# Slots ahead of weights, later embeddings, and squares, gates and scalings elsewhere, in a fused retention and mixture-of-experts kernel

## The chip, the cores and the metric

The kernel runs on one core of a Trainium2 chip. A core has TensorE (PE: matrix products, with its weight loads as PEld), VectorE (DVE), ScalarE (ACT), GpSimd (POOL) and SyncE (SP), which mostly issues DMAs. Each engine takes its own instructions in order and waits on semaphores for the others. The metric is the time of one execution on the device in microseconds (us); less is better.

## The reference

```
def _attn_ref(q, k, v):                       # 4 x 8 x 768 x 64
    gamma = 1.0 - 2.0 ** (-5.0 - arange(H)); scale = 1 / sqrt(D)
    for t in range(S):
        state = gamma * state + k[t] (x) v[t]
        y[t] = scale * q[t] @ state

def _moe_ref(x, expert_emb, tau, w1, w2):     # N, D, E, F = 3072, 512, 8, 1024
    xn = x / (norm(x) + 1e-6); en = expert_emb / (norm(expert_emb) + 1e-6)
    logits = xn @ en.T / tau
    expert_idx = argmax(logits, axis=1)
    probs = exp(logits - logits.max()); probs /= probs.sum() + 1e-9
    for e in range(E):
        h = maximum(x[mask e] @ w1[e], 0)
        out[mask e] = probs[expert e] * (h @ w2[e])

x = attention output, heads side by side, as (batch * sequence) x 512
```

All inputs and the output are float32.

## The kernel before

**Retention.** The recurrence is done in blocks of 256 tokens: 4 batches of 3 blocks are the 12 turns `m` of one loop (L718). k and q of a block are scaled by powers of gamma (`scale_k`, `scale_q`, on GpSimd, two blocks ahead) and transposed on TensorE (`transpose_k`, `transpose_q`, copied out by ScalarE into `kT`, `qT`). `scores` multiplies them, `masks` multiplies the scores by a causal mask on VectorE (`pm`), `inter` adds what comes from the running state and `intra` the product of `pm` and v (L410). `take` copies the result to `yT`, `rows` transposes it on VectorE and writes it to `xd` in memory in four DMAs. The buffers `pt` (two of them) take all transposes and small products.

**Routing, beside it.** One turn later `logits_products` multiplies `yT` by the normalised expert embeddings `enT`, which `expert_emb` makes in steps (norm on VectorE with a power on GpSimd, scaling, four small transposes on TensorE at L607, a copy to `enT`). The blocks are in six groups (`GROUPS`); at the end of a group `sums` and `choose` find the best expert of each token, `count` and `ranks` its slot, and `place` writes one record per token (row of x, row of the output, shifted logits) to the table `tbl` by indirect DMAs of GpSimd, one per 128 tokens (L529). Expert 0 starts early: its first 288 slots (`EARLY`) are filled from the first nine blocks alone, read to `tb` (`early_slots`), and their rows gathered from `xd` into `xge` (`early_gather`). The rest, `LATE`, are gathered into `xr0` after the last block.

**Experts.** Products are done with split operands: every float32 operand is a high part of type float32r and a low part, and three products are added (high by high, low by high, high by low). The eight weight pieces of an expert (four of w1, four of w2, 512 KB each) are loaded by SP into `raw` buffers (`load_piece`; three buffers, in order) and split by `split`: ScalarE casts the high part `whi` (L210), VectorE, sometimes GpSimd, subtracts for the low part `wlo` (L215). `LOADS` and `SPLITS` say in which blocks the first pieces are loaded and split. The rows of an expert are gathered to `xr` (`gather_rows`, one buffer), written to `xs` in memory (`write_rows`), read back in another order to `xg` (`read_quarters`), and then quarter by quarter transposed on VectorE (`x_turn`), cast on ScalarE (`xh`, L923) and subtracted (`xl`, L929, `x_low`). The norm of each row comes from `squares` on ScalarE, the factor `gt` of its output from `gates`, small steps on VectorE with a power on GpSimd and an exponential on ScalarE.

The loop over experts (L1092) has a first layer of eight tiles `ft` (12 products each, L228, then `hidden`: the activation to `hh` on ScalarE, the low part `hl` on VectorE) and a second layer: experts up to 4 in four column groups (L939), turned by `y_turn` and written to `og` by sixteen small DMAs (`out_rows`, L951) in the next expert's first layer; experts 5 to 7 in three row groups (L981). `finish` multiplies by `gt` and GpSimd scatters the rows to the output (L963). Splits, loads, squares and gates of the next expert are placed by hand at numbered tiles: the order in which the code is written is the order on every engine. For expert 0, the late rows pass the first layer as rows (L1014, output `hr`) and are then transposed.

## Time and profile before

| what | us |
|---|---|
| three timed runs | 452.30, 455.42, 456.49 (median 455.42) |
| the profiled execution | 450.94 |
| its span, first to last instruction | 449.1 |
| TensorE busy | 411.2 |
| VectorE, ScalarE, GpSimd busy | 255.5, 173.8, 168.7 |

The mean granted TensorE clock was 0.975 of the full one. Busy time of TensorE is modelled and overlaps between products, so a full stage doesn't mean that the array is at its peak. A stage is best read by who ended TensorE's waits in it, and the clock of a stage by its own row. Times in the rows are counted from the first instruction.

### The profile page before, as it was taken

The numbers are of one execution on the slowest core, as the hardware profiler recorded it, in microseconds if no ns is written. First come the engines' busy times: TensorE is split into PE (matmuls) and PEld (weight loads), VectorE is DVE, ScalarE is ACT, GpSimd is POOL, SyncE is SP. The second block draws the span as 40 slices with busy tenths as digits, with TensorE's granted clock in tenths as the row PEclk, the third lists the DMA queues.
The fourth block names the chain that finished last, engine by engine and source line by source line (L and its number), as shares of the span: only waits on it lengthen the run. The fifth ranks groups of instructions, "written<-read, shape, count | busy, mean of one in ns | idle before, by whom it ended". The sixth has DMA issues, their size and how long they took to land.

```text
span 449.1 us, 11335 instructions
## 1 busy us (share of the span) xinstructions
PE 411.2 (92%) x4540; PEld 367.0 (82%) x4540; DVE 255.5 (57%) x543; ACT 173.8 (39%) x315; POOL 168.7 (38%) x171
## 2 busy tenths in 40 slices
PE   7889889998859979997999999999998997999993
PEld 4778767877636978896899999999998987989982
DVE  3454745655862925565856585378467558666410
ACT  3314333334342515345346346156237326525300
POOL 1743356665645242072440172143135065012011
PEclk9989999999996999999899999999999999999998
DMA  9998878888583468649886968778788697864001
GB/s 238 274 227 217 224 196 228 222 217 200 131 228 112 99 165 234 151 122 279 233 267 176 229 220 243 165 254 268 177 242 273 178 290 256 257 203 138 0 26 47
DMA packets 97966, 88.75 MB, mean 198 GB/s; under 512 B 11148, under 2 KB 79644, under 8 KB 97904
## 3 DMA queue, kind: packets, MB, share of 16 engines
q1 hardware_dynamic: 92832, 74.85, 62.6%
q0 software_dynamic: 4928, 13.04, 8.4%
q8 instruction: 37, 0.61, 0.6%
q14 instruction: 25, 0.20, 0.2%
q10 hardware_dynamic: 144, 0.05, 0.1%
HBM read 65.27 MB, written 18.87 MB: 187 GB/s over the span
## 4 chain that ended last, share of the span: by engine, by line
PE 38%; DMA 16%; SPq 15%; DVE 10%; issue 10%; POOL 6%; ACT 4%; POOLq 0%; DVEq 0%; ACTq 0%
SPq L951 8%; PE py L410 5%; DMA xg<-xs 5%; PE py L981 5%; PE psc L228 4%; PE pt L330 4%; PE pst L228 4%; DMA xr<-xd,gi 4%; PE psc L357 4%; DVE wlo L215 3%; PE py L228 3%; DMA xs<-xr 2%; PE psc L939 2%; ACT whi L210 2%; SPq L912 2%
## 5 line engine op out<-in xcount | busy, mean ns | idle before, releaser
L215 DVE TENSOR_TENSOR wlo<-raw,whi 128x1024 fp32r<-128x1024 f32 x61 | 73.8, 1213 | 24.4 <-ACT whi L210 23.6
L963 POOL DMA_INDIRECT out_dram<-og,si x29 | 35.8, 1234 | 118.5 <-DVE og L956 101.7
L210 ACT CAST whi<-raw 128x1024 fp32r<-128x1024 f32 x64 | 65.6, 1043 | 6.2 <-POOL si L556 5.3
L366 DVE TENSOR_TENSOR pm<-psc,cst 128x512 f32<-128x512 f32 x48 | 30.9, 686 | 34.8 <-PE psc L357 34.8
L923 ACT CAST xh<-xt 128x384 fp32r<-128x384 f32 (+4 forms) x28 | 14.5, 522 | 73.2 <-DVE xt L922 73.2
L318 POOL TENSOR_TENSOR hl<-wlo,cst 128x512 f32<-128x512 f32 x22 | 22.9, 1062 | 51.1 <-PE pt L451 29.5
L559 POOL DMA_INDIRECT xr<-xd,gi x26 | 34.7, 1336 | 8.5 <-issue 5.5
L228 PE MATMUL pst<-xl,whi 128*128 128x384 f32 (+5 forms) x96 | 32.9, 343 | 4.0 <-DVE xl L929 4.0
L357 PE MATMUL psc<-qT,kT 64*64 64x128 f32 x768 | 35.1, 282 | 1.2 <-DVE qT L346 0.9
L247 POOL TENSOR_TENSOR r<-r,half 128x4 f32<-128x4 f32 (+1 forms) x9 | 8.9, 993 | 67.1 <-DVE r L246 67.1
L228 PE MATMUL pst<-xh,whi 128*128 128x384 f32 (+5 forms) x96 | 32.7, 341 | 1.3 <-ACT whi L210 1.2
L228 PE MATMUL pst<-xh,wlo 128*128 128x384 f32 (+5 forms) x96 | 32.4, 338 | 0.0
L529 POOL DMA_INDIRECT tbl<-zt,sloti x24 | 24.7, 1028 | 14.1 <-issue 5.8
L357 PEld LDWEIGHTS psc<-qT,kT 64*64 64x64 f32 x768 | 25.2, 136 | 5.3 <-DVE parts L459 1.5
L228 PE MATMUL py<-xh,whi 128*128 128x384 f32 (+5 forms) x84 | 28.5, 339 | 0.0
L228 PE MATMUL py<-xl,whi 128*128 128x384 f32 (+5 forms) x84 | 28.4, 338 | 0.0
L228 PE MATMUL py<-xh,wlo 128*128 128x384 f32 (+5 forms) x84 | 28.3, 337 | 0.0
L939 PE MATMUL psc<-hh,whi 128*128 128x288 f32 (+4 forms) x80 | 27.5, 344 | 0.0
L922 DVE STREAM_TRANSPOSE xt<-xg 128x416 f32<-128x416 f32 (+1 forms) x28 | 15.5, 573 | 21.0 <-DMA xg<-xs 20.1
L939 PE MATMUL psc<-hl,whi 128*128 128x288 f32 (+4 forms) x80 | 27.2, 340 | 0.0
L939 PE MATMUL psc<-hh,wlo 128*128 128x288 f32 (+4 forms) x80 | 27.2, 339 | 0.0
L228 PE MATMUL psc<-xh,whi 128*128 128x384 f32 (+5 forms) x76 | 25.4, 334 | 0.0
(207 smaller groups left out, 1019.4 us busy)
## 6 DMA issues: line engine op xcount, KB each, us to landing
raw<-in_moe_w_dram SPq DMA_DIRECT2D x46, 512.0 KB
raw<-in_moe_w_dram SPq DMA_DIRECT2D x28, 256.0 KB
xd<-x SPq DMA_DIRECT2D x48, 128.0 KB
...
```

Of the source, the lines that this page charges most:

```text
L210: nc.scalar.copy(out=hv, in_=rv)
L215: eng.tensor_tensor(out=lv, in0=rv, in1=hv.bitcast(F32), op=ALU.subtract)
L228: nc.tensor.matmul(acc[:, :w], a[:, f], x[:, kt, cols], start=(n == 0), stop=(n == 3 * KT - 1))
L318: return eng.tensor_tensor(out=dst[:, h], in0=src[m % 3][:, h, s], in1=w[:, h], op=ALU.mult)
L357: nc.tensor.matmul(psc[a][u * 64:(u + 1) * 64, j], kTs[m][a * D:(a + 1) * D, sk, j, u * 64:(u + 1) * 64], q_cols(m, a, j, u), start=True, ...
L366: i = nc.vector.tensor_tensor(out=pm, in0=psc[a], in1=C("mask")[:, sk * P:(sk + 1) * P].unsqueeze(1).broadcast_to([P, KT, P]), op=ALU.mult)
L410: nc.tensor.matmul(pys[m][u][o * D:(o + 1) * D, j], lhsT, rhs, start=first, stop=True, skip_group_check=True)
L529: i = nc.gpsimd.indirect_dma_start(out=tbl[:, :], out_offset=bass.IndirectOffsetOnAxis(ap=sloti[:, n:n + 1], axis=0), in_=zt[:, n], in_off ...
L559: nc.gpsimd.indirect_dma_start(out=xr[:n, j, :], out_offset=None, in_=xd[:rows_, :], in_offset=bass.IndirectOffsetOnAxis(ap=gi[:n, e, at:a ...
L939: nc.tensor.matmul(acc[:, :c], a[:, f], x[:, kt, :c], start=(n == 0), stop=(n == 3 * FT - 1))
L951: nc.sync.dma_start(out=og[h * Q:(h + 1) * Q, :n, i * P:(i + 1) * P], in_=yt[i * Q:(i + 1) * Q, h:nb:NQ].rearrange("p n t a -> p n (t a)"))
L963: i = nc.gpsimd.indirect_dma_start(out=out[:, :], out_offset=bass.IndirectOffsetOnAxis(ap=si[:n, e, j:j + 1], axis=0), in_=og[:n, j, :], i ...
```

## The change

It moves instructions and changes a few engines. Nothing is computed differently.

- **Embeddings:** the first steps of `expert_emb` run at the ends of blocks 0 and 1, the transposes in block 2, where the logits of blocks 0 and 1 are both made.
- **Slot writes:** `place` takes 2, then 3, then 4 columns a block instead of 2 and then 4.
- **Low parts of weights** in blocks 9 to 11 come after `choose`, `intra` and `take`; one goes to GpSimd in block 10. A fourth `raw` buffer; `LOADS` and `SPLITS` move one load and drop one split.
- **First rows of expert 0:** their transposes stand behind both `intra` of block 11.
- **After the last block:** slots are written before the last rows; the slots of the late rows and of experts 1 and 2 are read before any further weight is loaded; the first weight of expert 1 waits for the gather of the late rows.
- **Expert 0's second layer** does three column groups before the late rows instead of two.
- **Experts:** squares in the second layer of the expert before (at its first two groups), gates in the expert's own first layer, five splits in the first layer and three in the second (was four and four), the last two quarters of the next rows ahead of a split, output scaling on ScalarE, the gather of the expert after next at the second group for all experts.

TensorE between the retention and expert 0 (`pt` with `parts` are block 11's sums, `xge` the transposes of the gathered rows, `py` the products with `pm`). Before:

```order
L469 MATMUL pt<-parts,cst_61 32x32 x4
L577 MATMUL pst_2512<-ident,xge 128x128 x2
L577 MATMUL pst_2512<-ident,xge 128x32
L577 MATMUL pst_2518<-ident,xge 128x128 x2
L577 MATMUL pst_2518<-ident,xge 128x32
L577 MATMUL pt<-ident,xge 128x128 x2
L577 MATMUL pt<-ident,xge 128x32
L577 MATMUL pt<-ident,xge 128x128 x2
L577 MATMUL pt<-ident,xge 128x32
L410 MATMUL py_2428<-pm_2485,wlo 64x128
L410 MATMUL py_2428<-pm_2487,wlo 64x128
```

After:

```order
L412 MATMUL py_2427<-pm_2440,wlo 64x128
L412 MATMUL py_2427<-pm_2442,wlo 64x128
L579 MATMUL pst_2562<-ident,xge 128x128 x2
L579 MATMUL pst_2562<-ident,xge 128x32
L579 MATMUL pst_2568<-ident,xge 128x128 x2
L579 MATMUL pst_2568<-ident,xge 128x32
L579 MATMUL pt<-ident,xge 128x128 x2
L579 MATMUL pt<-ident,xge 128x32
L579 MATMUL pt<-ident,xge 128x128 x2
L579 MATMUL pt<-ident,xge 128x32
L233 MATMUL psc_2595<-xh,whi 128x288
```

The eight transposes stood between the sums and the products with `pm`; now the last products stand ahead of them, and the first layer's product with `whi` comes right behind.

SP's queue after the last block (`xd` is the write of block 11's rows, `tb` a read of slots, `raw` a weight piece, `TENSOR_LOAD` the reading of an expert's number). Before:

```order
L440 DMA xd<-x 256x1x128 x4
L169 TENSOR_LOAD cnti
L169 ISA x2
L188 ISA
L188 DMA raw<-in_moe_w_dram 128x1024
L1173 TENSOR_LOAD cnti
L1173 ISA x2
L186 ISA
L186 DMA raw<-in_moe_w_dram 64x1024
L186 ISA
L186 DMA raw<-in_moe_w_dram 64x1024
L857 DMA tb<-tbl 128x10
```

After:

```order
L172 TENSOR_LOAD cnti
L172 ISA x2
L838 ISA
L838 DMA tb<-tbl 128x4x10
L172 TENSOR_LOAD cnti
L172 ISA x2
L838 ISA
L838 DMA tb<-tbl 128x4x10
L1166 TENSOR_LOAD cnti
L1166 ISA x2
L191 ISA
L191 DMA raw<-in_moe_w_dram 128x1024
```

Three parts of two weights stood ahead of the first read of slots; now that read stands ahead of these rows, the two others in them, and the first weight comes last.

ScalarE in the first layer of expert 1 (`hh` are its activations, `sq` squares of expert 2's rows before, `whi` casts of weights, `zx` the exponential of the gates). Before:

```order
L234 ACTIVATE hh<-pst_3186 128x416
L234 ACTIVATE hh<-py_3218 128x416
L210 CAST whi<-raw 128x8x4x32
L262 ACTIVATE sq,ssq<-xr 128x512 x2
L234 ACTIVATE hh<-py_3235 128x416
L262 ACTIVATE sq,ssq<-xr 128x512
L262 ACTIVATE sq,ssq<-xr 32x512
L234 ACTIVATE hh<-psc_3261 128x416
L210 CAST whi<-raw 128x8x4x32
L234 ACTIVATE hh<-psc_3285 128x416
L234 ACTIVATE hh<-pst_3310 128x416
L210 CAST whi<-raw 128x1024
```

After:

```order
L215 CAST whi<-raw 128x8x4x32
L239 ACTIVATE hh<-pst_3168 128x416
L215 CAST whi<-raw 128x8x4x32
L239 ACTIVATE hh<-py_3200 128x416
L239 ACTIVATE hh<-py_3228 128x416
L215 CAST whi<-raw 128x8x4x32
L239 ACTIVATE hh<-psc_3243 128x416
L239 ACTIVATE hh<-psc_3272 128x416
L215 CAST whi<-raw 128x8x4x32
L282 ACTIVATE zx<-ze 128x32
L239 ACTIVATE hh<-pst_3290 128x416
L215 CAST whi<-raw 128x1024
```

The squares are gone from between the activations; the exponential, now of expert 1's own gates, stands a tile earlier.

The diff (`after` adds a dependency of one instruction on another):

```diff
@@ -51,4 +51,4 @@
 FILL = 512
-LOADS = (8, 8, 9, 9, 10, 10, 11, 11)
-SPLITS = (9, 9, 10, 10, 11, 11)
+LOADS = (8, 8, 9, 9, 9, 11, 11, 11)
+SPLITS = (9, 9, 10, 10, 11)
 STRIDE = 3200
@@ -143,3 +143,3 @@
     wp = ctxw.enter_context(tc.tile_pool(name="wp", bufs=9))
-    rp = ctxw.enter_context(tc.tile_pool(name="rp", bufs=3))
+    rp = ctxw.enter_context(tc.tile_pool(name="rp", bufs=4))
     hp = ctxw.enter_context(tc.tile_pool(name="hp", bufs=1))
@@ -167,2 +167,5 @@
 
+    def after(i, o):
+        tc.add_manual_dep(i.ins, o.ins.name, SYNC, reason="pace")
+
     def load_expert(s):
@@ -170,3 +173,3 @@
 
-    def load_piece():
+    def load_piece(behind=None):
         g = nload[0]
@@ -187,3 +190,5 @@
         elif j < 4:
-            nc.sync.dma_start(out=r, in_=w1r[ds(e * DM + j * P, P), :])
+            i = nc.sync.dma_start(out=r, in_=w1r[ds(e * DM + j * P, P), :])
+            if behind is not None:
+                after(i, behind)
         else:
@@ -332,5 +337,2 @@
 
-    def after(i, o):
-        tc.add_manual_dep(i.ins, o.ins.name, SYNC, reason="pace")
-
     def transpose_k(m, s, ps=None, copy=nc.scalar.copy):
@@ -558,3 +560,3 @@
     def gather(xr, n, j, e, at, rows_=NT):
-        nc.gpsimd.indirect_dma_start(
+        return nc.gpsimd.indirect_dma_start(
             out=xr[:n, j, :], out_offset=None, in_=xd[:rows_, :],
@@ -749,3 +751,3 @@
             nc.gpsimd.tensor_copy(out=zt[:, :, :2], in_=C("ids").rearrange("p (n o) -> p n o", o=2))
-        n = 4 if m >= NM - 3 else 2
+        n = 2 if m < 7 else 3 if m < 9 else 4
         place(ready[:n])
@@ -759,7 +761,7 @@
             transpose_k(m + 1, 1)
-        if m == 1:
+        if m == 2:
             next(emb_steps)
-        if m:
-            pl = logits_products(m - 1)
-            logits_rows(m - 1, pl)
+        for i in () if m < 2 else (0, 1) if m == 2 else (m - 1,):
+            pl = logits_products(i)
+            logits_rows(i, pl)
         if nxt:
@@ -787,4 +789,3 @@
             state_sums(m + 1)
-        if m == 0:
-            next(emb_steps)
+        if m < 2:
             next(emb_steps)
@@ -792,4 +793,4 @@
             nc.vector.memset(xge, 0.0)
-        for low in lows:
-            low(nc.vector if nxt else nc.gpsimd)
+        if m == NM - 2:
+            lows.pop()(nc.gpsimd)
         if m == NM - 1:
@@ -797,4 +798,2 @@
             run_all(add_counts(done))
-            for kt in range(KT):
-                rows_T(xge, EROWS, kt, slice(0, EARLY), bank(f"pst{kt}") if kt < 2 else None)
         intra(m, 1)
@@ -810,2 +809,7 @@
         take(m)
+        if m == NM - 1:
+            for kt in range(KT):
+                rows_T(xge, EROWS, kt, slice(0, EARLY), bank(f"pst{kt}") if kt < 2 else None)
+        for low in lows:
+            low()
         for _ in range(LOADS.count(m)):
@@ -843,4 +847,3 @@
     run_all(add_counts(g))
-    rows(m)
-    run(12)
+    run(9)
     pr = count(g)
@@ -850,2 +853,3 @@
     place(range(span(g).start, span(g).stop))
+    rows(m)
     for _ in range(9):
@@ -853,7 +857,5 @@
         run(1)
-    load_expert(1)
-    load_piece()
-    load_piece()
     nc.sync.dma_start(out=tb[:, 0, 3], in_=tbl[EARLY:CAPS[0], :])
     slots(1)
+    slots(2)
     for _ in sort_steps:
@@ -863,6 +865,6 @@
     split()
-    load_piece()
-    slots(2)
     for j, n in EROWS:
         square(xge, n, j, j)
+    run(12)
+    split()
     run(DF)
@@ -955,3 +957,3 @@
         o = og[:n, j]
-        nc.vector.tensor_scalar(out=o, in0=o if src is None else src, scalar1=gt[:n, e, j:j + 1], scalar2=None, op0=ALU.mult)
+        nc.scalar.activation(out=o, in_=o if src is None else src, func=AF.Copy, scale=gt[:n, e, j:j + 1])
         put_rows(e, j, n, og)
@@ -989,3 +991,3 @@
     indices(P, 0, slice(3, 4))
-    gather(xr0, P, 0, 0, 3)
+    late_rows = gather(xr0, P, 0, 0, 3)
     indices(P, 1, slice(0, NG))
@@ -994,3 +996,6 @@
     tokens(P, 1, slice(0, NG))
-    for dt in range(2):
+    load_piece(late_rows)
+    for _ in range(3):
+        load_piece()
+    for dt in range(3):
         acc = layer2(0, dt, hh0, hl0, EARLY)
@@ -1001,3 +1006,2 @@
     split()
-    load_piece()
     square(xr0, P, 0, 3)
@@ -1018,10 +1022,8 @@
             split()
-            load_piece()
             run_all(gsteps)
     read_quarters(1)
-    acc = layer2(0, 2, hh0, hl0, EARLY)
-    split()
     load_piece()
-    y_turn(2, acc, yt0, EARLY)
-    for f in range(2):
+    load_piece()
+
+    def turn_hidden(f):
         ps = pt_()
@@ -1033,3 +1035,8 @@
         nc.vector.tensor_tensor(out=hl0[:, kk, late], in0=o, in1=hh0[:, kk, late].bitcast(F32), op=ALU.subtract)
+
+    turn_hidden(0)
+    split()
+    load_piece()
     acc = layer2(0, 3, hh0, hl0, EARLY)
+    turn_hidden(1)
     split()
@@ -1049,7 +1056,2 @@
     squares(1)
-    gsteps = gates_of(1)
-    next(gsteps)
-    split(nc.gpsimd)
-    load_piece()
-    run_all(gsteps)
     indices(P, 2, slice(0, NG))
@@ -1071,15 +1073,13 @@
             lo()
-            load_piece()
         elif i == 1:
             x_low(e, 1)
-            lo = split_cast()
             x_turn(e, 2)
-            lo()
+            lo = split_cast()
             x_low(e, 2)
-            load_piece()
-        else:
             x_turn(e, 3)
-            split()
+            lo()
+        else:
             x_low(e, 3)
-            load_piece()
+            split()
+        load_piece()
 
@@ -1109,3 +1109,3 @@
                 nc.gpsimd.drain()
-            if ft % 2 == 0:
+            if ft in (0, 1, 3, 5, 6):
                 split()
@@ -1114,13 +1114,10 @@
                 out_rows(pend[1], pend[2], ft, pend[3])
-            if nxt:
-                if ft in (2, 3):
-                    squares(e + 1, ft - 2)
-                if ft == 3:
-                    read_quarters(e + 1)
-                if ft == 4:
-                    gsteps = gates_of(e + 1)
-                    next(gsteps)
-                if ft >= 6:
-                    for _ in range(4):
-                        next(gsteps, None)
+            if nxt and ft == 3:
+                read_quarters(e + 1)
+            if ft == 1:
+                gsteps = gates_of(e)
+                next(gsteps)
+            if ft > 2:
+                for _ in range(3):
+                    next(gsteps, None)
             if ft == FT - 2 and c % P:
@@ -1146,8 +1143,6 @@
                     finish_two()
+                if dt < 2:
+                    squares(e + 1, dt)
                 if dt < 3:
                     next_x(e + 1, dt)
-                else:
-                    split()
-                    load_piece()
-                    run_all(gsteps)
                 if dt == 1:
@@ -1161,9 +1156,7 @@
                 if nxt:
+                    if j < 2:
+                        squares(e + 1, j)
                     next_x(e + 1, j)
-                    if j == 0:
+                    if j == 1:
                         next_rows(e + 2)
-                    if j == 2:
-                        split()
-                        load_piece()
-                        run_all(gsteps)
                 finish(e, j, n, og, acc[:n])
```

## Rows read from the trace of the kernel before

**Rows 1.** Waits of TensorE over the whole span: line and tile, who ended the wait, us in total, how often, the longest.

```profile
PE pst L577 <- DMA xge<-xd,gi: 5.0, 2, 4.7
PE pst L228 <- DVE xl L929: 4.0, 4, 1.3
...
PE py L939 <- DVE hl L235: 2.7, 4, 1.4
PE pt L577 <- DMA xr<-xd,gi: 1.8, 1, 1.8
```

**Rows 2.** Busy time by stage: from and to (us), the length, then busy us and instructions of TensorE, its weight loads, VectorE, ScalarE and GpSimd, the mean granted TensorE clock (1.00 is 2.4 GHz), the share of the DMA engines and what they moved. The stages are: the end of block 1; from block 11's sums to the first layer of expert 0; the second layer of expert 0; experts 1, 2, 4, 5, 6 and 7.

```profile
23.00:31.00 8.00, 6.16 (x133) 5.21 (x133) 5.40 (x14) 1.17 (x2) 4.05 (x4) 0.79 1.07 257
130.00:143.14 13.14, 8.11 (x93) 5.47 (x89) 4.94 (x17) 3.69 (x6) 6.79 (x6) 0.61 0.66 220
157.40:187.00 29.60, 27.23 (x158) 24.23 (x157) 13.30 (x33) 9.24 (x19) 7.82 (x10) 0.94 0.76 203
187.00:230.36 43.36, 40.00 (x193) 36.86 (x192) 28.65 (x56) 21.95 (x42) 21.02 (x19) 0.96 0.73 205
230.36:265.78 35.42, 35.42 (x194) 35.42 (x193) 21.13 (x42) 15.41 (x29) 8.76 (x8) 1.00 0.76 211
300.76:336.35 35.59, 34.39 (x193) 34.07 (x193) 22.50 (x46) 15.47 (x27) 11.99 (x9) 1.00 0.83 233
336.35:371.81 35.46, 34.09 (x169) 30.34 (x169) 21.65 (x41) 15.49 (x27) 15.54 (x16) 1.00 0.83 250
371.81:408.42 36.61, 34.09 (x170) 30.34 (x169) 25.02 (x43) 18.76 (x31) 7.91 (x7) 1.00 0.69 214
408.42:442.10 33.68, 33.68 (x169) 30.20 (x167) 10.57 (x17) 5.81 (x10) 3.67 (x3) 1.00 0.16 53
```

**Rows 3.** Timeline of TensorE, then of VectorE, at blocks 1 and 2: start and length in us, line, operation, tiles and shape, how many merged, and in brackets the idle time before and what ended it.

```profile
24.50 0.44 PE L607 MATMUL pt<-ident,xge 8*128 8x8 f32 x4 [1.03 <-ACT kT L340]
...
26.32 0.66 PE L330 MATMUL pt<-ident,hh 128*128 128x128 f32 x4
26.90 0.71 PE L357 MATMUL psc<-qT,kT 64*64 64x128 f32 x8
...
30.95 0.65 PE L330 MATMUL pt<-ident,hh 128*128 128x128 f32 x4
...
37.47 0.45 PE L357 MATMUL psc<-qT,kT 64*64 64x128 f32 x8
...
39.88 0.66 PE L330 MATMUL pt<-ident,hh 128*128 128x128 f32 x4
...
22.95 0.15 DVE L249 RECIPROCAL r<-r 8x1 f32<-8x1 f32 x1 [3.48 <-POOL r L247]
```

**Rows 4.** Timeline of TensorE, then of VectorE, at the end of block 9 and the start of block 10.

```profile
115.17 0.18 PE L496 MATMUL pt<-cum,ones 128*128 128x16 f16 x1 [0.70 <-DVE zt L481]
115.78 0.17 PE L498 MATMUL pt<-oh,tri 128*128 128x16 f16 x1 [0.43 <-DVE oh L489]
...
112.45 2.36 DVE L215 TENSOR_TENSOR wlo<-raw,whi 128x1024 fp32r<-128x1024 f32 x2 [1.13 <-ACT whi L210]
```

**Rows 5.** Timeline of TensorE between block 11 and expert 0, then of VectorE, then of SP's DMA queue, a step of the chain that ended last (start, length, what), and a line of the page's groups (count, busy us, mean ns of one, idle before).

```profile
130.10 0.27 PE L469 MATMUL pt<-parts,cst 128*32 128x32 f32 x8
135.06 0.47 PE L577 MATMUL pst<-ident,xge 128*128 128x128 f32 x1 [4.69 <-DMA xge<-xd,gi]
...
139.16 1.98 PE L410 MATMUL py<-pm,wlo 64*64 64x128 f32 x32
...
143.14 0.40 PE L228 MATMUL psc<-xh,whi 128*128 128x288 f32 x1
...
130.05 1.29 DVE L366 TENSOR_TENSOR pm<-psc,cst 128x512 f32<-128x512 f32 x2
...
127.30 1.09 SPq L191 DMA_DIRECT2D raw<-in_moe_w_dram  x2
...
130.47 5.82 DMA xge<-xd,gi
...
L529 POOL DMA_INDIRECT tbl<-zt,sloti x24 | 24.7, 1028 | 14.1 <-issue 5.8
```

**Rows 6.** Timeline of TensorE, the products of expert 0's late rows: the first, the ninth and the last of 24.

```profile
167.07 0.77 PE L1014 MATMUL py<-whi,xh 128*128 128x512 f32 x1
...
170.49 0.39 PE L1014 MATMUL py<-wlo,xh 128*128 128x512 f32 x1
...
173.96 0.39 PE L1014 MATMUL py<-wlo,xh 128*128 128x512 f32 x1
```

**Rows 7.** Timeline of ScalarE in the first layer of expert 1.

```profile
206.40 0.63 ACT L262 ACTIVATE sq<-xr 32x512 bf16<-32x512 f32 x1 [1.08 <-DMA xr<-xd,gi]
```

**Rows 8.** Timeline of SP's DMA queue, then of VectorE, in the second layer of expert 3.

```profile
285.58 2.96 SPq L912 DMA_DIRECT2D xg<-xs  x4
...
292.35 1.11 DVE L922 STREAM_TRANSPOSE xt<-xg 128x416 f32<-128x416 f32 x2 [3.10 <-DMA xg<-xs]
...
302.14 1.22 DVE L215 TENSOR_TENSOR wlo<-raw,whi 128x1024 fp32r<-128x1024 f32 x1 [1.54 <-ACT whi L210]
303.29 0.56 DVE L929 TENSOR_TENSOR xl<-xt,xh 128x392 fp32r<-128x392 f32 x1
```

**Rows 9.** Timeline of VectorE at the end of the program.

```profile
442.19 0.75 DVE L956 TENSOR_SCALAR og<-py,gt 128x512 f32<-128x512 f32 x1 [4.82 <-PE py L981]
```

8 lines of the change are left out of this document (4 added, 4 removed).

## The prediction

> **What bounds the kernel now.** I read the waits of TensorE first [rows 1], then its busy time and granted clock by stage [rows 2], and last the timeline around each wait [rows 3 to 8]. The reader is to see that TensorE sets the end: in the stages of experts 2 and 7 it is busy for the whole stretch [rows 2], and elsewhere each wait names another engine or a transfer. The idle time is in few places: the first gathered rows of expert 0 (5.0 us), the low parts of the next expert's rows `xl` (4.0), the low parts of the hidden layer `hl` (2.7), the late rows of expert 0 (1.8) [rows 1]. Four of the stages have a mean granted clock under 1: it stood at its lower level, 1.2 GHz, for part of the stretch, after TensorE had been waiting [rows 2]. So a wait that goes may give back more than its own length. The profiled execution took 450.94 us with a span of 449.1; the median of the runs is 455.42, 4.5 above it. I make the sum in differences and take it off the median.
>
> **A. Embeddings one block later.** In block 0 VectorE starts the norm of the embeddings and then stands 3.48 us until GpSimd's power returns; the first masks of block 1 are queued behind it. TensorE then idles 1.03 us before the embedding transposes at 24.50 and goes on with the transposes of q at 26.32 [rows 3]. The changed kernel drops all of that from block 1: 26.32 - 24.50 + 1.03 = 2.8 us. Then the clock: scores to state products took 30.95 - 26.90 = 4.05 us, and the same instructions 39.88 - 37.47 = 2.41 us in the next block [rows 3], while the mean clock of this stretch was 0.79 [rows 2]. If TensorE isn't idle before, 1.6 us more. What is added: block 2 now has the embedding transposes, the wait for `enT` behind two masks, and the products of two blocks instead of one, which share two buffers. In block 1 the stretch from the embedding transposes to the end of the products took 26.32 - 24.50 = 1.8 us with its wait, which bounds the addition from above; nothing to 1.8, and I take 1.1, since four of the products stood in block 2 already. Net -3.3 (ends: -4.4 and -1.0; the lower one if the loads, which fill the DMA engines to a share of 1.07 in this stretch [rows 2], hold block 2 instead).
>
> **B. Low halves behind the choice.** At block 9 two low halves hold VectorE for 2.36 us and `choose` follows them; TensorE's counts wait 0.70 and 0.43 us for it [rows 4]. In the new order the choice is ahead. The halves now push the masks of block 10 instead, but by less than they pushed the counts. -1.1 (0 to -1.3).
>
> **C. First rows of expert 0.** TensorE ends block 11's sums at 130.10, gets the gathered rows at 135.06 after 4.69 us of idling, transposes them until 139.16, at the lower clock (0.61 in this stretch [rows 2]), does the 64 products with `pm` until 143.14 and starts the first layer [rows 5]. After the change the products come first. They need the second masks, which end at 130.05 + 1.29 = 131.3, a wait that block 11 hid so far: +1.0. Then 4.0 us of products and, at the full clock, 12 transposes: four of the size 128x128 take 0.66 us [rows 3], four of the 12 are narrow, so 1.8 us. 131.3 + 4.0 + 1.8 = 137.1 against 143.14: -6.0. The casts of `yT` and `xh` on ScalarE and the low parts on VectorE run a step behind the transposes, as the first layer takes them quarter by quarter. The gather must have landed by 135.3. The last of the three landed 5.82 us after its issue, at 136.3, with two raw loads issued from 127.30 on, just ahead of it [rows 5]. These loads are gone from there, and the queue of GpSimd has two slot writes less ahead of the gathers, 1.03 us each [rows 5]; both together need to win only 1.0 us. -6.0 (ends: -6.0 and -2.0, the latter if it lands no sooner than before and the clock falls again).
>
> **D. Late rows of expert 0.** The wait for `xr0` is 1.8 us [rows 1] and after it the clock is low: the first eight of 24 products of the late rows took 170.49 - 167.07 = 3.42 us, the other fifteen steps 173.96 - 170.49 = 3.47, or 0.231 each [rows 6]. Eight at that pace are 1.85: 1.6 us lost. The change puts a third output column group (24 matmuls) ahead of these rows, reads the slots ahead of the weights on SP's queue, and starts the whole chain earlier because of C. -3.4 (ends: -3.4, 0). The four weights of expert 1 now wait for the gather of `xr0` and stand ahead of the rows `xs`, `xg` of expert 1 on SP. No row shows that these rows still land in time; 1.0 us below and a rival are for that.
>
> **E. Expert 1.** Its stage takes 43.36 us, that of expert 2 35.42 for 408 columns instead of 416 [rows 2], so 36.1 would do: 7.2 us too many. ScalarE stands in the first layer for squares of rows that the gather has not brought: the last, at 206.40, waited 1.08 us for its rows [rows 7], and the activations behind it in ScalarE's order waited too; `hl` follows from them, and TensorE waits for `hl` [rows 1]. The squares move to the second layer of the expert before, where their rows landed long ago, the gates to the expert's own first layer. -7.2 (to -3.5 if part of the clock's loss stays).
>
> **F. Experts 4, 5 and 6.** Stage times 35.59, 35.46 and 36.61 against 33.68 for the undisturbed last one with 384 columns (34.4 for 392) [rows 2]: 1.2 + 1.8 + 2.9 = 5.9 us. The reason: `xg` reached VectorE only at 292.35, and the last `xl` came at 303.29 behind a low half that itself waited 1.54 us for ScalarE [rows 8], while TensorE was in the next expert since 300.76. The change helps twice: `xl` of the last quarter goes ahead of its split, and VectorE loses the output scalings and one split there. -5.9 (to -2).
>
> **ScalarE's new work.** Four scalings per expert. A square of 512 elements took 0.63 us there [rows 7], VectorE 0.75 for the last scaling out of PSUM [rows 9]; I bound the new one by half and by twice the square and take 0.63, the row on its own engine. Four of them and four squares, 5.0 us, lie beside a second layer that is about half of a stage of 35: nothing on the path, and -0.1 at the end. The Trainium skill speaks against this edit: ScalarE: Activation LUTs, "Rules for kernel authors", wants multiplications on VectorE, and its timing formula with one pointer operand gives, as an estimate from that page, 0.71 us for 512 elements. The 0.63 of the row is near that. By that rule the edit costs what the last rival below says; by the row it is free as long as ScalarE has room, and it is busy for about half of a stage or less [rows 2].
>
> **Sum.** 3.3 + 1.1 + 6.0 + 3.4 + 7.2 + 5.9 = 26.9. I put 2 against it, 1.0 for expert 1's rows and 1.0 for waits that surface when the rest moves: -25. 455.4 - 25 = **430** us, about 426 for an execution like the profiled one.
>
> **Rivals.** *Next rows late as before.* SP is in order: in the first layer it issues 16 small copies, raw loads that wait for a free buffer, `xs`, `xg`; `xg` was issued at 285.58 only [rows 8]. The diff adds one more raw load ahead of it and moves the gather of the expert after next behind the squares. If F is lost and half of E: 455.4 - 25 + 5.9 + 3.6 = 440. For it: that queue. Against: fewer waits for the squares, a fourth raw buffer, and `xl` no longer last on VectorE. *Expert 1's rows land late*, behind four weight loads on SP: as in the first rows of expert 0, 4.7 us of waiting and 1.6 of clock at its start, 436. *Weights late.* One piece less is split ahead of each expert. If each of seven second layers waits 3 us for a split, 21 us come back: 451, no change to speak of. Against: ScalarE and VectorE have room, and the last split stands two tiles ahead of the end of the first layer. *Slower: a loop over ScalarE.* Squares stand ahead of the casts `xh`, the next gather waits for the squares to free its tile, its rows go through `xs` and `xg`, and the next casts wait for those. If the loop takes longer than an expert, every boundary waits. From `xg` to the end of the last `xl` the old order took 303.29 + 0.56 - 292.35 = 11.5 us, with its waits, and TensorE lost about 1.2 us with `xg` 300.76 - 292.35 = 8.4 us ahead of the next expert [rows 2, 8]. The change is slower than before when the six boundaries from expert 1 on lose over 27 / 6 = 4.5 us each; at 11.5 us that is with `xg` landing under 5.1 us ahead. At 6 us each: 455.4 - 25 + 36 = 466. Against: the squares no longer wait for a gather, so the loop starts earlier.
>
> **How the numbers follow.** Forecast 0.62, next rows late 0.16, expert 1 late 0.10, weights late 0.07, loop over ScalarE 0.05. Lower end: all terms whole, no new wait, and a median that lies like the lowest run: 424. Upper end: the first two rivals and the short ends of A, C and D, 445; the last two stay out. About 1% is what a measurement of this kernel can tell from no change. Faster by over 1% (the first three): 0.88; within 1%: 0.07; slower: 0.05.
>
> **What the profile after would show.** No half-clock stretch in block 1 (A); counts of block 10 without a wait (B); first layer of expert 0 some 10 us earlier with no wait for `xge` but one for `pm` (C); no wait for `xr0` (D); stage of expert 1 near 36 us (E); no wait for `xl` at the later boundaries (F). The forecast is wrong if TensorE waits for `xl` at expert 1 or at every boundary, or for `whi` or `wlo` in the second layers.

## The result and the profile after

The changed kernel took 436.4 us (median of 4 runs) against 454.3 for the kernel before in the same session (455.42 in the runs shown above): a ratio of 0.956, interval 0.948 to 0.965. Ratios here and below are of the fast runs alone; two of the four timed runs, 439.51 and 439.62, lie over 1.5% above the fastest, and the profiled one is the first of them. A second session, on a chip where both were slower, gave 445.5 against 466.0, 0.952 (0.945 to 0.960). So the change gives 4 to 5%, 18 to 22 us, where 25 were forecast; 430 was too low, the range held.

The profiled execution after took 439.51 us, its span 437.7. TensorE's waits in it, to be held against [rows 1] (line and tile, who ended the wait, us in total, how often, the longest):

```profile
PE pt L500 <- DVE oh L491: 2.4, 1, 2.4
...
PE pst L233 <- ACT xh L925: 1.4, 1, 1.4
PE pst L233 <- DVE wlo L220: 1.4, 2, 0.7
...
PE pst L233 <- DVE xl L931: 1.0, 3, 0.5
```

The waits for gathered rows, 5.0 and 1.8 us in [rows 1], and that for `hl`, 2.7, are gone, and that for `xl` fell from 4.0 to 1.0. New are 2.4 us for `oh`, a step of the choice at the end of block 11, 1.4 for `xh` and 1.4 for low halves `wlo`. The stages, as in [rows 2]: from the sums of block 11 to the first layer of expert 0; second layer and late rows of expert 0; experts 1, 2, 4, 5 and 6.

```profile
130.00:140.50 10.50, 7.53 (x94) 4.92 (x90) 6.84 (x16) 2.17 (x5) 7.51 (x8) 0.66 0.88 257
156.25:183.88 27.63, 25.67 (x158) 22.90 (x156) 13.41 (x32) 8.96 (x20) 7.04 (x10) 1.00 0.83 211
183.88:222.22 38.34, 37.36 (x193) 35.82 (x193) 20.62 (x40) 20.76 (x41) 11.54 (x12) 1.00 0.79 217
222.22:259.35 37.13, 36.32 (x194) 35.35 (x193) 22.99 (x45) 20.42 (x36) 13.25 (x13) 1.00 0.85 232
294.33:330.03 35.70, 34.88 (x193) 34.09 (x193) 23.72 (x47) 20.56 (x34) 11.35 (x12) 1.00 0.85 244
330.03:363.59 33.56, 33.56 (x169) 30.38 (x169) 20.02 (x37) 18.16 (x32) 9.47 (x10) 1.00 0.86 251
363.59:397.16 33.57, 33.57 (x169) 30.39 (x168) 19.76 (x35) 17.44 (x30) 9.88 (x9) 1.00 0.88 251
```

Expert 1 fell from 43.36 to 38.34, experts 4 to 6 from 107.66 to 102.83. Expert 2 rose from 35.42 to 37.13. The first stretch still runs at a mean clock of 0.66, where it was 0.61 before.

Each run below leaves its own trace; one stage of it tells more than its time. For the retention (block 0 to the start of block 11) took 115.5 us before, 115.7 after, and 116.0 to 128.1 in twelve other traces that hardly differ there, and that spread hides anything under some 5 us. Much of it goes with the chip: 124.7 to 128.1 in the four traces of the one on which `again` ran, 116.0 to 120.7 in the eight of two others. So stages are compared, each counted from its own start.

| trace | blocks 0 to 3 | sums to first layer | first layer of 0 | to expert 1 | expert 1 | experts 2 to 6 | sums to the end |
|---|---|---|---|---|---|---|---|
| before | 44.6 | 13.0 | 14.2 | 29.7 | 43.3 | 178.1 | 319.0 |
| after | 45.6 | 10.4 | 15.8 | 27.6 | 38.3 | 174.9 | 307.6 |
| again | 43.5 | 5.7 | 15.2 | 27.4 | 38.3 | 172.9 | 300.6 |
| held_low | 45.1 | 5.7 | 14.5 | 27.1 | 39.6 | 171.7 | 299.1 |
| rows_first | 42.9 | 11.9 | 14.5 | 27.0 | 39.4 | 171.7 | 305.1 |
| no_wait | 44.0 | 6.6 | 15.3 | 26.1 | 37.4 | 174.0 | 299.9 |
| emb_early | 45.1 | 5.7 | 15.2 | 29.0 | 39.8 | 171.7 | 302.1 |
| squares_early | 42.8 | 10.6 | 16.2 | 26.8 | 38.3 | 171.7 | 304.4 |
| gates_back | 43.6 | 6.9 | 14.5 | 26.8 | 38.3 | 178.2 | 305.3 |
| sq_gates_before | 44.0 | 9.2 | 16.4 | 26.9 | 44.1 | 171.7 | 309.0 |
| finish_vector | 47.7 | 9.4 | 16.1 | 27.5 | 38.3 | 187.1 | 319.4 |
| x_order | 43.3 | 10.1 | 16.8 | 27.4 | 39.2 | 178.7 | 312.7 |
| chain | 43.0 | 9.7 | 15.8 | 27.6 | 38.3 | 171.7 | 303.7 |
| best | 43.5 | 5.7 | 14.5 | 26.1 | 37.0 | 171.7 | 295.7 |

The columns are us, from the starts of TensorE's instructions: first scores of block 0 to those of block 4; block 11's sums to the first layer of expert 0; that layer; its second layer and late rows; expert 1; experts 2 to 6 together; and all from block 11's sums to the last instruction. By the last column the change is worth 11.4 us behind the retention in its first trace and 18.3 in `again` (on another chip; the kernel before has one trace only), and nothing is seen of it in the retention.

### The profile page after: what moved, and what is told of

Its sections match the earlier page's. It is cut to its first block, busy times and chain, and to the rows that moved or that the text cites. A ratio compares the mean times of both kernels' runs of the same rounds, so it can differ in the third digit from the quotient of the medians.

```text
span 437.7 us, 11314 instructions
## 1 busy us (share of the span) xinstructions
PE 408.4 (93%) x4540; PEld 365.6 (84%) x4540; DVE 243.2 (56%) x517; ACT 191.5 (44%) x343; POOL 157.6 (36%) x169
## 4 chain that ended last, share of the span: by engine, by line
PE 47%; DMA 13%; issue 12%; SPq 11%; DVE 8%; ACT 4%; POOL 2%; POOLq 0%; DVEq 0%; ACTq 0%
PE py L412 8%; SPq L953 5%; PE pt L335 5%; PE py L233 5%; PE psc L359 5%; PE pst L233 5%; PE psc L233 5%; PE py L983 4%; PE psc L983 4%; DMA xr<-xd,gi 4%; DMA xg<-xs 3%; DMA xs<-xr 3%; PE pst L384 2%; DVE wlo L220 2%; DMA raw<-in_moe_w_dram 2%
## 5 line engine op out<-in xcount | busy, mean ns | idle before, releaser
L220 DVE TENSOR_TENSOR wlo<-raw,whi 128x1024 fp32r<-128x1024 f32 x63 | 76.6, 1218 | 22.5 <-ACT whi L215 21.4
L965 POOL DMA_INDIRECT out_dram<-og,si x29 | 29.4, 1015 | 154.7 <-ACT og L958 100.3
L368 DVE TENSOR_TENSOR pm<-psc,cst 128x512 f32<-128x512 f32 x48 | 30.9, 686 | 39.7 <-PE psc L359 39.6
L924 DVE STREAM_TRANSPOSE xt<-xg 128x416 f32<-128x416 f32 (+1 forms) x28 | 15.8, 582 | 47.7 <-DMA xg<-xs 47.7
L531 POOL DMA_INDIRECT tbl<-zt,sloti x24 | 24.9, 1039 | 14.7 <-DVE sloti L522 8.8
L925 ACT CAST xh<-xt 128x384 fp32r<-128x384 f32 (+4 forms) x28 | 14.5, 520 | 29.8 <-DVE xt L924 29.8
L233 PE MATMUL psc<-xh,wlo 128*128 128x384 f32 (+5 forms) x76 | 25.8, 339 | 0.0
L233 PE MATMUL psc<-xl,whi 128*128 128x384 f32 (+5 forms) x76 | 25.8, 339 | 0.0
L434 ACT COPY yT<-py 128x512 f32<-128x512 f32 x24 | 12.9, 589 | 27.1 <-PE py L412 25.5
L941 PE MATMUL psc<-hh,whi 128*128 128x416 f32 (+4 forms) x72 | 24.6, 341 | 0.0
```

The costliest lines, as they stand in the source:

```text
L220: eng.tensor_tensor(out=lv, in0=rv, in1=hv.bitcast(F32), op=ALU.subtract)
L233: nc.tensor.matmul(acc[:, :w], a[:, f], x[:, kt, cols], start=(n == 0), stop=(n == 3 * KT - 1))
L368: i = nc.vector.tensor_tensor(out=pm, in0=psc[a], in1=C("mask")[:, sk * P:(sk + 1) * P].unsqueeze(1).broadcast_to([P, KT, P]), op=ALU.mult)
L531: i = nc.gpsimd.indirect_dma_start(out=tbl[:, :], out_offset=bass.IndirectOffsetOnAxis(ap=sloti[:, n:n + 1], axis=0), in_=zt[:, n], in_off ...
L941: nc.tensor.matmul(acc[:, :c], a[:, f], x[:, kt, :c], start=(n == 0), stop=(n == 3 * FT - 1))
L965: i = nc.gpsimd.indirect_dma_start(out=out[:, :], out_offset=bass.IndirectOffsetOnAxis(ap=si[:n, e, j:j + 1], axis=0), in_=og[:n, j, :], i ...
```

## The experiments

All start from the changed kernel, unless said. Ratios are to the kernel before.

**The same kernel again** (`again`, no edit).

> The changed kernel itself once more. If the waits found in its first trace belong to the kernel, they come again at the same places: 2.4 us of TensorE before block 11's counts, about 1.6 us ahead of the first product of expert 1 and 1.6 us more for xl in its first tile, 0.95 us for a low half of a weight (wlo) in the first tile of experts 2 and 4. If they are chance, they move. Time 431 to 440 us, as its four runs so far.

Measured: 445.5 us, ratio 0.952. The wait for `xh` ahead of expert 1 came again (1.2 us), that for `xl` too (1.0); 2.4 us for `oh` and the low half at expert 2 did not, so these two differ between executions of the same code; at expert 4 a stop of 0.7 us stands at the same product again. What decides about `oh`, the next run shows.

**Low half on VectorE** (`held_low`).

```
         if m == NM - 2:
-            lows.pop()(nc.gpsimd)
+            held = lows.pop()
...
             run_all(ranks(done, pr))
+            held()
             place(range(span(done).start, span(done).stop))
```

> The low half that the change gives to GpSimd in block 10 runs on VectorE instead, in block 11 behind the ranks. Theory: this GpSimd subtraction (2.35 us) holds VectorE's instruction w of the choice, which took 2.78 us instead of 0.19, and so TensorE's counts; without it the counts come at once, the first layer of expert 0 starts near 137 instead of 140.5, its first products no longer run at half the clock (1.8 us), and the time falls by 4 to 5.5 us. Rival: the gathered rows xge, which landed at 134.51, only take the place of that wait, and the clock falls all the same: 0.5 to 2 us less.

VectorE, then GpSimd, then TensorE of the changed kernel at the end of block 11 (`w` and `oh` are steps of the choice, `wlo` the low half):

```profile
131.46 0.19 DVE L483 TENSOR_TENSOR zt<-pt,m 128x32 f32<-128x32 f32 x1
131.68 2.78 DVE L486 SCALAR_TENSOR_TENSOR w<-zt,cst 128x32 f32<-128x32 f32 x1
...
134.72 0.19 DVE L491 TENSOR_TENSOR oh<-w,wmn 128x32 f16<-128x32 f32 x1
```

```profile
132.06 2.35 POOL L220 TENSOR_TENSOR wlo<-raw,whi 128x1024 fp32r<-128x1024 f32 x1
```

```profile
132.41 0.19 PE L498 MATMUL pt<-cum,ones 128*128 128x32 f16 x1
134.97 0.19 PE L500 MATMUL pt<-oh,tri 128*128 128x32 f16 x1 [2.37 <-DVE oh L491]
...
135.14 1.99 PE L412 MATMUL py<-pm,wlo 64*64 64x128 f32 x32
137.06 1.79 PE L579 MATMUL pst<-ident,xge 128*128 128x128 f32 x6
...
140.50 0.61 PE L233 MATMUL psc<-xh,whi 128*128 128x288 f32 x1
```

`w` took 2.78 us and ended at 134.46, less than 0.1 us after GpSimd's subtraction. TensorE stood 2.37 us, the next 32 products took 2 us at half the clock (1.1 at the full one, 131.38) and so did the transposes. In the traces of `chain`, `squares_early` and `x_order`, where GpSimd began a little later, it was `oh` that took 2.7 to 3.0 us; in `again`, `no_wait` and `emb_early`, where it had ended before the choice, nothing was held. `w`, `oh` and the subtraction each read two operands from SBUF, the engines' on-chip memory. An instruction with only one operand there was not held, as `gates_back` shows, VectorE first and then GpSimd:

```profile
136.15 0.19 DVE L483 TENSOR_TENSOR zt<-pt,m 128x32 f32<-128x32 f32 x1
136.37 1.38 DVE L486 SCALAR_TENSOR_TENSOR w<-zt,cst 128x32 f32<-128x32 f32 x1
```

```profile
135.34 2.36 POOL L220 TENSOR_TENSOR wlo<-raw,whi 128x1024 fp32r<-128x1024 f32 x1
```

`zt`, whose `pt` lies in PSUM, the memory that TensorE writes to, ran in 0.19 us within the subtraction; `w` was held until its end. In the kernel before the same was to be seen, and missed: `r<-r,ssq` took 2.13 us beside such a subtraction, at 193.30. `held_low`, VectorE and then TensorE:

```profile
142.89 0.19 DVE L486 SCALAR_TENSOR_TENSOR w<-zt,cst 128x32 f32<-128x32 f32 x1
```

```profile
143.66 0.18 PE L500 MATMUL pt<-oh,tri 128*128 128x32 f16 x1
...
144.86 1.15 PE L579 MATMUL pst<-ident,xge 128*128 128x128 f32 x6
...
147.03 0.40 PE L233 MATMUL psc<-xh,whi 128*128 128x288 f32 x1
```

From the sums to the first layer it is 5.7 us instead of 10.4, and the first layer, at the full clock, 14.5 instead of 15.8: 6.0 less. But in `again`, on the same chip, GpSimd was early, and there it is 5.7 too. So the time, 446.2 us (0.957), is that of `again`: the edit takes away a loss that the changed kernel has in some executions (whole in four of the nine other traces that keep this code, in part in two), of 5 to 6 us when whole. The Trainium skill, SBUF — State Buffer, section "Who interferes with whom", says that VectorE with two SBUF inputs and a GpSimd instruction that reads SBUF exclude each other for a whole instruction; these traces agree.

**Rows first** (`rows_first`, from `held_low`): `rows_T` of `xge` again right behind `add_counts`, ahead of both `intra`.

> From the run with the low half on VectorE: the transposes of expert 0's gathered rows stand again ahead of the last products of the retention. Theory (term C without GpSimd's hold): TensorE waits for the gathered rows behind the sums, 3 to 4.5 us, and the clock falls behind that wait: the stretch from the last scores to the second layer of expert 0, 25.3 to 25.6 us in the two runs with the low half on VectorE, takes 4 to 6 us more. Rival: the gather lands as the masks end, and the order gives under 1.5 us.

```profile
131.54 0.27 PE L471 MATMUL pt<-parts,cst 128*32 128x32 f32 x8
134.18 0.33 PE L579 MATMUL pst<-ident,xge 128*128 128x128 f32 x1 [2.37 <-DMA xge<-xd,gi]
135.63 0.33 PE L579 MATMUL pst<-ident,xge 128*128 128x128 f32 x1 [1.12 <-DMA xge<-xd,gi]
137.04 1.17 PE L579 MATMUL pst<-ident,xge 32*128 32x32 f32 x4 [1.08 <-DMA xge<-xd,gi]
...
139.86 1.99 PE L412 MATMUL py<-pm,wlo 64*64 64x128 f32 x32
```

TensorE waits 2.37, 1.12 and 1.08 us for the three gathers, and the products with `pm` come behind at half the clock. From the sums to the first layer it is 11.9 us against 5.7: 6.2 more, where term C had 6.0. The time, 439.7 us on another chip, has a ratio of 0.961 against 0.957 for `held_low`; the intervals overlap, so the 6 us are shown by the stage alone.

**No wait of the weights** (`no_wait`): `load_piece(late_rows)` becomes `load_piece()`.

> The first weight of expert 1 no longer waits for the gather of the late rows; nothing else. Theory: with the wait, the DMA engines stand nearly idle until 158 (share 0.26 from 145 to 158) and then carry the weights and the rows of expert 1 at once, so that its rows xg land at 182.5, too late by some 3 us. Without it they land 2 to 4 us earlier and the time falls by 2 to 3 us; the late rows, which landed 6 us ahead of their use, still come in time. Rival: SP's queue and the rows' own way through memory set xg, not the weights: no change, or the late rows come late: up to 2 us more.

SP, VectorE and TensorE ahead of expert 1, first of `again`, the same chip, then of `no_wait`:

```profile
166.97 0.36 SPq L191 DMA_DIRECT2D raw<-in_moe_w_dram  x1
...
182.19 2.50 SPq L914 DMA_DIRECT2D xg<-xs  x4
```

```profile
189.53 1.10 DVE L924 STREAM_TRANSPOSE xt<-xg 128x416 f32<-128x416 f32 x2 [2.61 <-DMA xg<-xs]
```

```profile
190.82 0.46 PE L233 MATMUL pst<-xh,whi 128*128 128x416 f32 x1 [1.19 <-ACT xh L925]
```

```profile
162.91 0.35 SPq L191 DMA_DIRECT2D raw<-in_moe_w_dram  x1
...
180.06 2.38 SPq L914 DMA_DIRECT2D xg<-xs  x4
```

```profile
186.87 1.10 DVE L924 STREAM_TRANSPOSE xt<-xg 128x416 f32<-128x416 f32 x2 [0.29 <-DMA xg<-xs]
```

```profile
189.13 0.35 PE L233 MATMUL pst<-xh,whi 128*128 128x416 f32 x1
```

Counted from the start of expert 0's second layer (163.38 and 163.04), the first weight is issued 3.7 us earlier, `xg` 1.8, and VectorE waits 0.29 us for it instead of 2.61; TensorE goes on at 189.13 without a wait. Way to expert 1 and its stage: 63.5 us instead of 65.8. In time 444.5 against 445.5, inside the intervals. `best` against `chain`, below, shows the stages once more: 63.1 against 65.9.

**Embeddings early** (`emb_early`): first steps at the end of block 0 and transposes in block 1, logits of one block a turn, as before.

> Only the embeddings go back: first steps at the end of block 0, transposes and products in block 1. The prediction had 3.3 us for this part, so 3.3 us more. What the trace of the changed kernel shows: block 1 gave back 2.2 us, but block 2 took 3.05 more, of which 1.5 for the transposes and products and 1.55 at half the clock behind a stall of TensorE's own queue. So this part is worth 0 to 1.5 us: with it undone, 0 to 1.5 us more in the stretch of blocks 1 and 2.

Blocks 0 to 3 took 45.1 us; with the embeddings late 42.8 to 47.7 in twelve traces, seven of them under 43.7. The expectation held: 1 us or so, no more than one stall of TensorE's own queue, which is what this text calls a stop in which the profile shows nothing waited for ("issue"). One trace cannot tell 1 us from none here. The time, 449.3, has a ratio of 0.961 (0.955 to 0.966). In it 2.8 us are a wait for `xh` ahead of expert 1, whose first products then run at half the clock.

**Squares early** (`squares_early`). In this kernel the gates of an expert read sums of squares of the next one, which changes the output; the amount of work is the same.

```
+            if nxt and ft in (2, 3):
+                squares(e + 1, ft - 2)
...
-                if dt < 2:
-                    squares(e + 1, dt)
...
-                    if j < 2:
-                        squares(e + 1, j)
                     next_x(e + 1, j)
-                    if j == 1:
+                    if j == 0:
                         next_rows(e + 2)
```

> Of the changed kernel only the squares go back into the first layer of the expert before (its third and fourth tile), with the gather after next at the first row group for experts 5 to 7; the gates stay. Theory (term E of the prediction): in expert 1's first layer ScalarE then stands for rows that the gather has not brought (issued about 7 us into the stage, landed 15 us into it), the activations and hl behind it come late, and the stage takes 4 to 6 us more than the 38.3 of the changed kernel. Where later gathers land after those tiles too, 0 to 2 us more at each of experts 2 to 4. Together 4 to 10 us more. Rival: expert 1's stage was cured by its rows coming earlier, not by the place of the squares: under 2 us more.

Expert 1's stage: 38.34 us, to the hundredth as in the changed kernel. The theory of term E fell: with the gates late, the place of the squares gives nothing there.

**Gates back** (`gates_back`), and **squares and gates as before** (`sq_gates_before`, that and the squares, and all gates in the first layer of the expert before).

```
     squares(1)
+    gsteps = gates_of(1)
+    next(gsteps)
+    split(nc.gpsimd)
+    load_piece()
+    run_all(gsteps)
     indices(P, 2, slice(0, NG))
...
-            if ft in (0, 1, 3, 5, 6):
+            if ft in (0, 1, 3, 5, 6)[e == 1:]:
...
-            if ft == 1:
+            if ft == 1 and e > 1:
```

The last two lines are of `gates_back` alone.

> From the changed kernel, only ahead of expert 1: the gates of expert 1 and one low half of a weight on GpSimd stand again between its squares and the gather of expert 2's rows; squares stay late. The squares alone, put back early, left expert 1's stage at 38.3 us. New theory: these steps are what made the stage long before: GpSimd's low half (2.4 us) and the gates' power hold the gather back by 3 us or more and VectorE's gate steps (2.1 us at one of them), ScalarE's exponential waits for those, and the activations behind it. Alone, without squares in ScalarE's way: 1 to 3 us more in expert 1's stage. Rival: they are nothing without the squares: under 0.5 us.

> As the run before this, and squares and gates of all experts back at their old places in the first layer of the expert before. Theory: the gather, now 3 us later, meets squares in ScalarE's first layer: expert 1's stage takes 4 to 6 us more than 38.3, as in the kernel before; the later boundaries stay within 1 us each, since the scalings are still on ScalarE. Together 4 to 7 us more. Rival: the other edits cover it: under 2 us.

GpSimd in `gates_back` (`gi` are the rows to gather), then its expert 2, then expert 1 of `sq_gates_before`, as in the rows of stages:

```profile
189.23 1.03 POOL L252 TENSOR_TENSOR r<-r,half 128x4 f32<-128x4 f32 x1 [18.33 <-DVE r L251]
190.22 2.40 POOL L220 TENSOR_TENSOR wlo<-raw,whi 128x1024 fp32r<-128x1024 f32 x1
...
193.22 1.16 POOL L561 DMA_INDIRECT xr<-xd,gi  x1 [0.28 <-POOL gi L555]
```

```profile
221.18:263.17 41.99, 39.48 (x194) 37.84 (x192) 26.98 (x51) 23.26 (x40) 16.76 (x16) 0.92 0.85 231
```

```profile
187.61:231.75 44.14, 41.24 (x193) 37.99 (x194) 27.75 (x54) 23.18 (x45) 18.80 (x19) 0.92 0.79 219
```

The power and the low half hold the gather from 189.2 to 193.2: in both runs it is issued 10.4 us into expert 1, and 6.8 us in the changed kernel and in `squares_early` (9.0 before). With the squares in the way the loss, 5.8 us, is in expert 1, as before; without them it is 6.6 us at expert 2, whose rows come late (`xg` reaches VectorE 4.1 us ahead of expert 2 instead of 6.3; TensorE's wait is for `whi` and `wlo` in the first tile, 2.4 us, and the clock falls, 0.92). The first expectation had 1 to 3 us and the wrong stage, the second was right in place and size. So what made expert 1 long is the late gather, and the place of the squares only decides which expert pays. The gates and the low half were put back together; no run separates them, though 2.4 of the 3.6 us are the low half by its row. In time the ratios are 0.971 (0.965 to 0.978) and 0.966 (0.960 to 0.972).

**Scalings on VectorE** (`finish_vector`): `finish` with `nc.vector.tensor_scalar`, as before.

> Only the output scalings go back from ScalarE to VectorE. Theory: VectorE's chain from the landing of xg to the last low half (9.3 us of work in 9.85) is what ends last at experts 2 and 4, so each pair of scalings in it costs up to 1.4 us at the boundaries with little lead: 1 to 4 us more. Rival, the rule that multiplications belong on VectorE: ScalarE waited 6.1 us for the output rows with the scalings at the head of its queue, ahead of the squares and casts; freed of them the next gather and the casts come earlier, and the time falls by 1 to 2 us.

455.8 us, ratio 0.993: this edit alone carries some 17 us, where the theory had 1 to 4 and the rival a gain. Behind the retention it is 12 to 19 by the last column. VectorE in the second layer of expert 5, TensorE in the first tile of expert 6, and expert 6 as in the rows of stages:

```profile
364.52 0.88 DVE L958 TENSOR_SCALAR og<-og,gt 128x512 f32<-128x512 f32 x2 [6.62 <-DMA og<-yt]
369.41 1.04 DVE L924 STREAM_TRANSPOSE xt<-xg 128x384 f32<-128x384 f32 x2 [4.01 <-DMA xg<-xs]
...
372.66 0.74 DVE L958 TENSOR_SCALAR og<-py,gt 128x512 f32<-128x512 f32 x1
373.32 0.86 DVE L958 TENSOR_SCALAR og<-og,gt 128x512 f32<-128x512 f32 x2
...
377.81 0.74 DVE L958 TENSOR_SCALAR og<-psc,gt 128x512 f32<-128x512 f32 x1
...
380.07 0.74 DVE L958 TENSOR_SCALAR og<-psc,gt 128x512 f32<-128x512 f32 x1
```

```profile
376.68 0.50 PE L233 MATMUL pst<-xh,whi 128*128 128x384 f32 x1 [1.36 <-ACT whi L215]
```

```profile
373.32:413.53 40.21, 37.37 (x169) 32.16 (x168) 27.18 (x48) 19.39 (x32) 13.66 (x13) 0.92 0.77 226
```

VectorE stands 6.6 us for the output copies, and 3.1 us of scalings come between `xg` and its last work for expert 6. ScalarE's casts wait for its transposes, and in experts 3 to 6 TensorE waits 4.3 us for low halves and 2.8 for casts. In expert 6 the clock falls as well, to a mean of 0.92 where it was 1.00 before [rows 2]. The rule on multiplications (ScalarE: Activation LUTs, "Rules for kernel authors", in the Trainium skill) would have had this the faster place; here a scaling out of SBUF is shorter on VectorE by itself, 0.44 us against 0.67 on ScalarE, and the kernel is slower with it there. Without the scalings' move the other edits would make experts 2 to 6 9 us slower than before (187.1 against 178.1).

**The order of the next rows** (`x_order`): in `next_x` the low halves of weights ahead of the last two quarters, as before.

> From the changed kernel, only the order on VectorE in the second layers goes back: low halves of weights ahead of the last two quarters of the next rows. The prediction gave this and the scalings 5.9 us together. Theory after the run with the scalings on VectorE (17 us at experts 3 to 6): the scalings carry the gain, and the order only chooses whether xl or wlo comes last: within 1 us at each boundary, -1 to 2 us in all. Rival: the order matters as predicted: 2 to 6 us more, with waits for xl in the first tiles of experts 4 to 7.

```profile
PE pst L233 <- DVE xl L931: 5.5, 8, 1.3
```

446.3 us, ratio 0.974; experts 2 to 6 take 178.7 us, 4 to 6 more than in the two traces of the changed kernel. The rival was right in size and my theory not: the order matters beside the scalings. The waits came in the first tiles of experts 2 to 6, 0.5 to 1.3 us each, where the rival had named 4 to 7.

**Second layers in another order** (`chain`).

```
+            if nxt and ft == 2:
+                read_quarters(e + 1)
             if pend and not pend[5] and ft < 4:
                 out_rows(pend[1], pend[2], ft, pend[3])
-            if nxt and ft == 3:
-                read_quarters(e + 1)
...
-                if dt < 2:
-                    finish_two()
-                if dt < 2:
-                    squares(e + 1, dt)
+                if dt == 0:
+                    split()
+                    squares(e + 1)
+                    next_rows(e + 2)
                 if dt < 3:
                     next_x(e + 1, dt)
-                if dt == 1:
-                    next_rows(e + 2)
+                if dt in (1, 2):
+                    finish_two()
```

(the same in the row groups; the first split leaves `next_x`)

> From the changed kernel: the rows xg of the next expert are read before the output copies of the third tile, all squares and the first split stand at the head of the second layer with the gather after next behind them, and the output scalings come one group later. Theory: SP's queue (output copies ahead of xg) and ScalarE's queue (scalings that wait for those copies, ahead of squares and casts) set how far ahead of the next expert xg lands, 6.5 to 9 us now; it becomes 10 us or more for experts 3 to 6, the waits for wlo in the first tiles of experts 2 and 4 go (0.95 and 0.4 us each): 1.5 to 3 us less. Rival: VectorE's work alone fills those boundaries, or the rows collide with weight loads: no change.

VectorE and ScalarE in the second layer of expert 3, the changed kernel first, then `chain`:

```profile
287.81 1.11 DVE L924 STREAM_TRANSPOSE xt<-xg 128x416 f32<-128x416 f32 x2 [9.65 <-DMA xg<-xs]
```

```profile
283.68 1.34 ACT L958 ACTIVATE og<-og,gt 128x512 f32<-128x512 f32 x2 [6.13 <-DMA og<-yt]
```

```profile
278.23 1.10 DVE L924 STREAM_TRANSPOSE xt<-xg 128x416 f32<-128x416 f32 x2
```

In the changed kernel ScalarE stood 6.13 us for the output copies with squares and casts queued behind, and VectorE 9.65 us for `xg`, until 6.5 us ahead of expert 4 (294.33). In `chain` it starts 14.7 us ahead (292.90) without a wait. Experts 2 to 6 take 171.7 us, with no wait. But so they do in `held_low`, `emb_early` and `rows_first`, whose code for them is that of the changed kernel, which took 174.9 and 172.9: the changed kernel stands at the edge with its lead, and loses 0 to 3 us from run to run. Time 436.4, ratio 0.949, within the interval of the changed kernel; what is shown is the lead, not a gain.

**All three** (`best`: `held_low`, `no_wait`, `chain`).

> Three edits of the changed kernel together: the low half of block 10 on VectorE behind block 11's ranks (3 to 5 us less, by its own run's trace), no wait of the first weight of expert 1 for the late rows (2.3 us less, by its trace), and the order of the run before this one in the second layers (1.5 to 3 us less). If they add up: 7 to 9 us under the changed kernel, a ratio to the kernel before of 0.935 to 0.942. If they share a cause, or run to run differences of the retention blocks cover them: 3 to 5 us.

430.2 us against 458.6: ratio 0.938 (0.930 to 0.945), under both sessions of the changed kernel, which was not run in this one. Each stage behind the retention has the best value of the table or shares it. Against the changed kernel's 0.952 to 0.956 that is some 7 us, as expected if the parts add up.

## Why the prediction was right, and where it was not

The direction and the range held, and of the places those behind the retention (C to F), not those in it (A and B). The profiled executions differ by 11 us, the medians by 19, as the one before lay 4.5 us under its median and the one after 3.1 above. C to F, less the 2 us set against them, were to give 20.5 us behind the retention; 11.4 came in the first trace and 18.3 in `again`. The prediction's own sign against it, a wait for `xl` at expert 1, came as well, but it cost 2 us there and not the forecast. The upper end of the range, 445, is the two first rivals added (430.4 + 9.5 + 5.3); with the short ends of A, C and D on top, which the text names too, the sum would be 455. By its own steps:

- **A**, -3.3: mis-sized. Blocks 0 to 3 took 44.6 us before and 45.6 after; with `emb_early` the part is worth about 1 us. The step that failed is that the clock's loss would go: the half clock that block 1 had there went (0.99 instead of 0.79 from 23 to 31 us), but a stall of TensorE's own queue came later in it, and the products behind took 3.5 us instead of 2.0, at a mean clock of 0.53. Block 2 took 10.4 us instead of 8.9, 1.4 more, where 1.1 was allowed. The products of block 1 before, then the stall and the products after:

```profile
31.53 1.98 PE L410 MATMUL py<-pm,wlo 64*64 64x128 f32 x64
```

```profile
29.79 0.34 PE L384 MATMUL pst<-whi,hl 64*64 64x64 f32 x8 [1.64 <-issue]
...
30.65 3.53 PE L412 MATMUL py<-pm,wlo 64*64 64x128 f32 x64
```

- **B**, -1.1: block 9 to block 10 took 10.90 us instead of 11.95, but a wait of 0.9 us remained ahead of the counts, for `kT` in a shared buffer, and blocks 9 and 10 together gained 0.2 us. Not told from chance.
- **C**, -6.0: right in size (6.2 by `rows_first`; 13.0 to 5.7 us in `again`), but in the first trace 13.0 went to 10.4 only and the first layer rose from 14.2 to 15.8: of 6.0, 1.1 came. GpSimd's low half in block 10 held the choice; the prediction has no term for it. The sum was also helped by an error: its 4.0 us for the products with `pm` come from a row at half the clock, and at the full one they and the small steps between took 2.9 (141.99 to 144.86 in `held_low`). With no hold the stretch is 7.3 us shorter than before.
- **D**, -3.4: 29.65 to 27.63 us, -2.0. The wait for `xr0` went. What is missing is the wait of 1.4 us for `xh` at the start of expert 1, for which 1.0 us was set aside. The rival that has expert 1's rows late behind the weights is half true, and `no_wait`, with 26.1 us, shows why: the change's own new wait.
- **E**, -7.2: -5.0; most of what is missing is the first tile of expert 1, which took 4.3 us where the next took 2.3, with three waits for `xl` (1.0 in all). The step that failed is the reason: the loss was put down to squares on ScalarE, and `squares_early` shows that they cost nothing when the gather is early. The gates and the low half that went from GpSimd, ahead of that gather, were the cause.
- **F**, -5.9: -4.8 (107.66 to 102.83). Both reasons were needed: with the scalings back these three experts took 114.9 us, with the order back 104.9. The lead of `xg` at expert 4 fell all the same, from 8.4 us [rows 8] to 6.5, and expert 4 took 35.7 us in the first trace, where eight others have 34.1.
- **Two us against new waits:** 2.4 for `oh`, 1.7 at expert 2, 1.4 ahead of expert 1 and 2.0 in its first tile came: 7.5 and some clock. The 1.7 at expert 2 is in no other trace of this code; what stands at expert 1 came once more in `again`.
- **ScalarE's new work** at nothing: right for the path, as `finish_vector` shows, at 0.67 us a scaling where 0.63 was taken; its wait for the output copies ahead of the squares was not seen.

Shown by runs: C's order, the hold, D's new wait, E's gates with the low half, F's two edits. Argued only: A, below its noise, and B. Not undone singly: the fourth `raw` buffer with the load and the split that moved, the slot writes, the slots read ahead of the weights, and the third column group ahead of the late rows.
